# One block of small products instead of two, and a second product put off by a step, in a recurrence fused with a feed-forward layer

## The chip, the core and the metric

The kernel runs on one core of a Trainium2 chip. What counts is the device time of one execution in microseconds. The kernel before was timed three times: 566.85, 567.27 and 568.79 us, median 567.27 us.

## What is computed

The first half is a gated linear recurrence over 768 tokens, for 4 batches of 8 heads with 48 features; the second half is a feed-forward layer of width 2048 with an ELU between its two products. All of it is fp32.

```python
for t in range(S):                       # S = 768; q, k, v, f_logit: (4, 8, 768, 48)
    state = f[:, :, t, :, None] * state + np.einsum('bhd,bhe->bhde', k[:, :, t], v[:, :, t])
    y[:, :, t] = np.einsum('bhd,bhde->bhe', q[:, :, t], state)
...
h = x @ w_in                             # x: y as (3072, 384); w_in: (384, 2048)
g = np.where(h > 0.0, h, alpha * (np.exp(np.minimum(h, 0.0)) - 1.0))
return (g @ w_out).astype(np.float32)    # w_out: (2048, 384)
```

f is the sigmoid of f_logit.

## The kernel before

The function `fast` does the work; `general` is a fallback that is entered only when a flag, computed on the way, says that the inputs are out of range. Tokens are worked in twelve units of 256 (three to a batch, so units 0, 3, 6 and 9 begin a sequence), heads in pairs, and a unit's tokens in four chunks of 64.

The order of every engine's instructions is written out by hand. Time is counted in steps T, 16 to a unit, 192 in all. A table `plan` says which pieces of the recurrence are issued at which step, and the main loop at the end of `fast` adds the feed-forward layer around them:

- At an even step, `up(P)` issues the first product for one of the eight pairs of 128 hidden features of a unit, P = T/2. From unit 1 on this is `up7`, a scheme with seven products instead of eight (L882); it writes two banks, pa and pb, of a pair of PSUM buffers named "h". ScalarE copies a part of pa (L889), VectorE adds it to the rest (L891), and VectorE finishes the ELU of the pair before (L936). GpSimd makes sums of it for the second product (L946).
- At an odd step, `joined(P)` combines pb with it on VectorE (L904) and starts the exponential on ScalarE (L914, L915). Then come the planned pieces, and then `down(P - LAG)`, LAG = 2, the second product (L981), which accumulates over a unit's eight pairs in four PSUM banks, m0 to m3. Its first product of a unit goes to m0. After the eighth pair ScalarE and VectorE put the output together from these banks (L992, then five instructions of L991), and four transfers store it.

The recurrence of unit u works ahead of the feed-forward layer of unit u - 1. For u from 3 on, with t = 16(u - 1), the tuple A3 = (2, 4, 5, 7, 9, 11) gives the steps after t at which these are issued:

1. `transposed`: keys are transposed by TensorE (L669) into the banks a0 and a1, and copied out by ScalarE.
2. `advance`: 32 products of 64x48 (L728, 64 records in the trace) form each chunk's contribution to the state, into a0 and a1.
3. `step`: VectorE adds the contributions to the state chunk by chunk (L686), and for the last chunk multiplies by the decay (L691). In the first unit of a sequence the first of them is a copy on ScalarE (L688); in the last unit of a sequence the last is left out.
4. `scores`: 32 products of 64x64 of queries and keys (L705), into a0 and a1 again; `mask`: two VectorE instructions multiply them by the causal mask (L713).
5. `outputs`: masked scores by values (L743), into a0 and a1.
6. `carried`: queries by state (L763) on top; ScalarE copies the result out as the input of the feed-forward layer.

Each of `advance`, `scores`, `outputs` and `carried` is issued after an `up` or before it, in between full 128x128 products; the small products use a quarter of TensorE's array each.

Beside this, VectorE computes the decays of the next unit (L626, L631), and from step 52 on reduces a piece of the reread weights every fourth step (L603). During the first 76 us weights arrive as 64-bit numbers and are converted by VectorE and ScalarE (L563, L567, L573, L581) before the products that need them. A tile `fine`, 128x3, holds the range flags of the decays; `watch(u)` (L650) updates it once for each unit, for unit 1 at step 3. `warm` (L1032) issues products of the identity that nobody reads, to fill a hole on TensorE.

Of the kernel before, what the change touches and what calls it, by code (L numbers as in the profile page):

```python
# [356 lines left out]
def fast(ctx: ExitStack, tc: tile.TileContext, q, k, v, f_logit, w_in, w_out, out, flag, outer):  # L357
# [18 lines left out]
    nc = tc.nc  # L376
# [7 lines left out]
    NC = U // C  # L384
    UPB = S // U
    NU = B * UPB
    HP = H // 2
    NFT = DFF // 128
# [5 lines left out]
    LAG = 2  # L394
    AHEAD = 7
    WA = 1
    F1 = (1, 3)
    W0 = 3
    HOLD = 2
    A1 = (2, 5, 6, 8, 10, 11)  # L400
    D2 = (16, 18, 20, 22)
    A2 = (23, 25, 25, 26, 27, 28)
    D3 = (-7, -5, -3, -1)
    A3 = (2, 4, 5, 7, 9, 11)
    BL = 13
    RR = 0
    MX = 10
# [254 lines left out]
    def transposed(u, h, bank, pairs=(0, 1)):  # L662

        if 0 in pairs:
            pts[u, h] = ps.tile([128, 2, NW, 128], FP32, tag=bank, name=f"psT{u}_{h}")
            kns[u, h] = sb.tile([128, 2, NW, 128], FP32, tag="kn", name=f"kn{u}_{h}")
        for p in pairs:
            for w in range(NW):
                nc.tensor.transpose(  # L669
                    pts[u, h][:, p, w], in_=qkf[u % NB]["k"][:, 2 * h + p, w * W : (w + 1) * W], identity=ident[:]  # L670
                )
        p = slice(pairs[0], pairs[-1] + 1)
        nc.scalar.copy(kns[u, h][:, p], pts[u, h][:, p])
# [3 lines left out]
    def step(u, c):  # L677

        if u % UPB == UPB - 1 and c == NC - 1:
            return  # L680
        new = pus[u][c % 2][:, c // 2]
        box = boxes[(u * NC + c) % len(boxes)]
        s = box[:].rearrange("n (p d) -> n p d", d=64)[:, 0:HP, PAD:]
        if u % UPB or c:
            old = sts[u, c][:].rearrange("n (p d) -> n p d", d=64)[:, 0:HP, PAD:]
            nc.vector.tensor_tensor(out=s, in0=new, in1=old, op=ALU.add)  # L686
        else:
            nc.scalar.copy(s, new)  # L688
        if c == NC - 1:
            end = qkf[u % NB]["f"][:, :, 1, U - 1 :].broadcast_to([128, HP, D])  # L690
            nc.vector.tensor_tensor(out=s, in0=s, in1=end, op=ALU.mult)  # L691
        sts[(u, c + 1) if c < NC - 1 else (u + 1, 0)] = box

    def scores(u, banks=("a0", "a1"), pairs=range(HP), pc=None):

        t = qkf[u % NB]
        if pc is None:
            ats[u] = sb.tile([128, 2, NW, HP, C], FP32, tag="at", name=f"at{u}", bufs=1)
            pc = [ps.tile([128, NW, HP, C], FP32, tag=banks[r], name=f"psS{u}_{r}") for r in range(2)]
        for p in pairs:  # L700
            for w in range(NW):
                for b in range(2):
                    cols = slice(w * W + b * C, w * W + b * C + C)
                    for r in range(2):
                        nc.tensor.matmul(  # L705
                            pc[r][FULL[b], w, p], lhsT=t["k"][FULL[r], p, cols], rhs=t["q"][FULL[r], p, cols],
                            start=True, stop=True,
                        )
        return pc

    def mask(u, pc):
        for r in range(2):
            nc.vector.tensor_tensor(  # L713
                out=ats[u][:, r].rearrange("k w p i -> k (w p) i"), in0=pc[r][:].rearrange("k w p i -> k (w p) i"),
                in1=twice[:].unsqueeze(1).broadcast_to([128, NW * HP, C]), op=ALU.mult,
            )

    def advance(u, pairs=range(HP)):

        if u not in pus:  # L720
            pus[u] = [ps.tile([128, NW, HP, D], FP32, tag=n, name=f"psU{u}_{n}") for n in ("a0", "a1")]
        pu = pus[u]
        for p in pairs:
            for w in range(NW):
                for r in range(2):
                    h = 2 * p + r
                    for b in range(2):
                        nc.tensor.matmul(  # L728
                            pu[b][FULL[r], w, p], lhsT=kns[u, p // 2][FULL[b], p % 2, w, FULL[r]],
                            rhs=vs[u % NB][FULL[b], w, PAD + h * D : PAD + (h + 1) * D],  # L730
                            start=(w == 0 and p == 0), stop=(w == NW - 1 and p == HP - 1), skip_group_check=True,
                        )

    def outputs(u, banks=("a0", "a1")):


        pys[u] = [ps.tile([128, NW, HP, C], FP32, tag=banks[b], name=f"psY{u}_{b}") for b in range(2)]
        at = ats.pop(u)
        for w in range(NW):
            for p in range(HP):  # L740
                for r in range(2):
                    for b in range(2):
                        nc.tensor.matmul(  # L743
                            pys[u][b][FULL[r ^ b], w, p], lhsT=of_head(u, b, w, r, p),
                            rhs=at[FULL[b], r, w, p], start=(w == 0 and p == 0), stop=False,
                            skip_group_check=True,
                        )

        for b in range(2):
            nc.scalar.copy(between[:], pys[u][b][:, :, :, 0])  # L750

    def carried(u):

        t = qkf[u % NB]
        py = pys.pop(u)
        for w in range(NW):
            for p in range(HP):
                for b in range(2):
                    c = 2 * w + b
                    if (u % UPB, c) == (0, 0):  # L760
                        continue
                    for r in range(2):
                        nc.tensor.matmul(  # L763
                            py[b][FULL[r ^ b], w, p], lhsT=sts[u, c][FULL[r], 64 * p + r * PAD : 64 * (p + 1) + r * PAD],
                            rhs=t["q"][FULL[r], p, c * C : (c + 1) * C],
                            start=False, stop=True, skip_group_check=True,
                        )
        x = xts[u] = sb.tile([128, HP + 1, U], FP32, tag="xt", name=f"xt{u}", bufs=3)
        to = x[:, 0:HP].rearrange("n p (w b i) -> n b w p i", b=2, i=C)
        nc.scalar.copy(to[:, 0], py[0][:])  # L770
        for r in range(2):
            nc.scalar.copy(to[FULL[r], 1], py[1][FULL[1 - r]])
        for r in range(2):
            frm = PAD + D * r
            (nc.sync if u > 1 else nc.scalar).dma_start(
                out=x[GAP[r] : GAP[r] + PAD, 0:NKT], in_=x[frm : frm + D, NKT]
            )
# [46 lines left out]
    def at_step(step, *todo):  # L824
        plan.setdefault(step, []).extend(todo)

    def attention(u, first, then):

        kept = []
        for p, i in enumerate(first):  # L830
            at_step(i, (lambda: settle(u)) if p == NKT else lambda p=p: decays(u, p))
        if u > 1:
            at_step(then[0], lambda: transposed(u, 0, "a0"), lambda: transposed(u, 1, "a1"))
        at_step(then[1], lambda: advance(u))
        at_step(then[2], *(lambda c=c: step(u, c) for c in range(NC)))
        at_step(then[3], lambda: kept.append(scores(u)), lambda: mask(u, kept[0]))
        at_step(then[4], lambda: outputs(u))
        at_step(then[5], lambda: carried(u))

    gs, ss, pms, phs = {}, {}, {}, {}  # L840

# [187 lines left out]
        nc.tensor.matmul(pf[0:1, :], lhsT=low[:], rhs=causal[:, W - 1 : W], start=True, stop=True)  # L1029
        nc.vector.tensor_copy(flag[:], pf[0:1, :])  # L1030

    def warm(n, bank="m0"):  # L1032

        pw = ps.tile([128, 4, 128], FP32, tag=bank, name="psW")
        for _ in range(n):
            nc.tensor.matmul(
                pw[:], lhsT=ident[:], rhs=ident[:].unsqueeze(1).broadcast_to([128, 4, 128]), start=True, stop=True
            )
# [81 lines left out]
    at_step(F1[1], lambda: move(1, 1, nc.scalar), lambda: watch(1))  # L1120
    at_step(F1[1] + 2, lambda: scale(1, ("q", NKT, nc.gpsimd)))
    at_step(A1[0], lambda: transposed(1, 0, "a0"), lambda: transposed(1, 1, "a1"))
    attention(1, (), A1)
    at_step(8, lambda: load(2))
    at_step(14, lambda: gates(2))
# [8 lines left out]
    for u in range(3, NU):  # L1134
        t = (u - 1) * NFT
        at_step(t + BL, lambda u=u: blend(u))
        at_step(t - 16, lambda u=u: load(u))
        at_step(t - 8, lambda u=u: gates(u))
        attention(u, [t + i for i in D3], [t + i for i in A3])
    for n in range(NR):  # L1140
        t = 3 * NFT + (NU - 4) * NFT * n // NR + RR
        at_step(t, lambda n=n: reread(n))
# [3 lines left out]
    for T in range(NU * NFT):  # L1146
        P = T // 2
        sevens = order[P][0] >= DIRECT
        if T % 2 and sevens:
            joined(P)  # L1150
        if T % 2 == 0 and P and order[P - 1][0] < DIRECT:
            elu(P - 1)
        for f in plan.pop(T, ()):
            f()
        if T % 2 == 0:
            up(P)
        elif P >= LAG:
            down(P - LAG)
        for n in later.pop(T, ()):
            split(n)  # L1160
            lower(n)
# [53 lines left out]
```

## Time and profile before

| | us |
|---|---|
| median of three runs | 567.27 |
| lowest, highest | 566.85, 568.79 |
| profiled execution, span from its first to its last instruction | 567.3 |
| TensorE busy in it | 547.5 (97%) |
| VectorE busy | 409.4 (72%) |
| GpSimd busy | 292.7 (52%) |
| ScalarE busy | 230.2 (41%) |

Nothing of the profiled execution's time is shown outside of its span, so the span stands for its own time. In the page's second part each digit is the busy share of one fortieth of the span, in tenths. In the timeline a row gives the start and the length in us, the engine, the line of the kernel, the operation, the tiles that it writes and reads, shapes, and how many instructions of that kind follow one another; in brackets stands the idle time of the engine before it and what ended it. Matmuls are pipelined and their ends are modelled, so durations on TensorE are best taken from start to start. An fp32 product appears as two records.

### The profile page before, as it was taken

The page shows a single profiled execution, that of the slowest core. Times are in us where ns is not written, and L with a number is a line of the kernel's source. Part 1 is how long each engine was busy: PE and PEld are TensorE (multiplying, and loading weights), DVE is VectorE, ACT ScalarE, POOL GpSimd, SP SyncE. Part 2 cuts the span into 40 slices and gives each one's busy share as a digit, 9 for nine tenths or more (in the row PEclk, how much of TensorE's full clock was granted, in tenths as well). Part 3 has the DMA queues.
Part 4 walks back from the last instruction along what each step waited for, and adds up shares of the span by engine and source line. Part 5 has one row for each costly group of instructions (what it writes and reads, how often), then busy time and mean ns, then how long its engine had stood idle before and what let it go on. Part 6 is the DMA issues. An engine that isn't in the chain of part 4 may idle for free.

```text
span 567.3 us, 15527 instructions
## 1 busy us (share of the span) xinstructions
PE 547.5 (97%) x6336; PEld 509.7 (90%) x6336; DVE 409.4 (72%) x802; ACT 230.2 (41%) x424; POOL 292.7 (52%) x567
## 2 busy tenths in 40 slices
PE   6879998999999999999999999999999999999996
PEld 3566677999999999999999999999999999999996
DVE  8779989785675785885785885786776876745543
ACT  3287862443343433434343343333343343233331
POOL 6601788475374465456366357257248348325332
PEclk9899999999999999999999999999999999999999
DMA  8997951024024225215216216206206203201001
GB/s 212 266 261 209 298 129 43 3 47 114 3 46 138 65 52 145 79 42 156 78 36 155 86 38 153 86 19 173 84 14 178 84 6 74 84 2 36 29 2 35
DMA packets 38193, 53.30 MB, mean 94 GB/s; under 512 B 3712, under 2 KB 27936, under 8 KB 38112
## 3 DMA queue, kind: packets, MB, share of 16 engines
q1 hardware_dynamic: 37312, 51.62, 34.2%
q8 instruction: 52, 0.85, 0.7%
q10 hardware_dynamic: 800, 0.59, 0.4%
q14 instruction: 29, 0.24, 0.1%
HBM read 44.04 MB, written 4.72 MB: 86 GB/s over the span
## 4 chain that ended last, share of the span: by engine, by line
PE 81%; DMA 7%; DVE 7%; issue 2%; POOL 1%; ACT 1%; SPq 0%; DVEq 0%; ACTq 0%; POOLq 0%
PE psH L882 36%; PE psM L981 36%; DMA area<-in_moe_w_in_dram 4%; PE psS L705 2%; PE psY L743 2%; PE psY L763 2%; PE psU_a L728 2%; DVE f L631 2%; PE psT L669 1%; DMA xt<-xt 1%; DMA f<-f 1%; DVE f L626 1%; DMA k<-in_k_dram 1%; DVE bits L563 1%; DVE area L850 1%
## 5 line engine op out<-in xcount | busy, mean ns | idle before, releaser
L882 PE MATMUL psH<-xt,wi 128*128 128x128 f32 (+1 forms) x1056 | 195.0, 294 | 0.1
L946 POOL TENSOR_TENSOR sums<-gg 128x128 f32<-128x128 f32 x176 | 77.7, 462 | 214.5 <-DVE gg L936 205.9
L882 PEld LDWEIGHTS psH<-xt,wi 128*128 128x128 f32 x1056 | 149.5, 192 | 1.8 <-DVE hh L891 0.4
L914 ACT ACTIVATE gg<-hh 128x512 f32<-128x512 f32 x88 | 55.5, 631 | 232.0 <-DVE hh L904 154.6
L882 PE MATMUL psH<-xt,area 128*128 128x128 f32 x704 | 121.8, 275 | 1.3 <-DVE hh L904 1.0
L882 PEld LDWEIGHTS psH<-xt,area 128*128 128x128 f32 x704 | 106.5, 191 | 6.3 <-PE psH L882 1.3
L891 DVE TENSOR_TENSOR hh<-psH,u 128x256 f32<-128x256 f32 x88 | 37.1, 422 | 93.9 <-ACT u L889 93.9
L981 PE MATMUL psM<-area,sums 128*128 128x192 f32 x528 | 100.2, 326 | 0.0
L981 PEld LDWEIGHTS psM<-area,sums 128*128 128x128 f32 x528 | 88.2, 190 | 0.0
L981 PE MATMUL psM<-wo,gg 128*128 128x192 f32 x352 | 74.9, 335 | 0.0
L631 DVE RECIPROCAL f<-f 128x256 f32<-128x256 f32 x36 | 62.7, 1747 | 1.1
L936 DVE SCALAR_TENSOR_TENSOR gg<-gg,hh 128x512 f32<-128x512 f32 x88 | 61.9, 703 | 1.5 <-ACT gg L915 1.5
L915 ACT ACTIVATE gg<-gg 128x512 f32<-128x512 f32 x96 | 60.6, 631 | 3.0
L981 PEld LDWEIGHTS psM<-wo,gg 128*128 128x128 f32 x352 | 55.2, 190 | 2.0
L904 DVE TENSOR_TENSOR hh<-psH,u43h 128x256 f32<-128x256 f32 (+1 forms) x176 | 54.7, 352 | 3.0
L946 POOL TENSOR_TENSOR sums<-gg,sums 128x128 f32<-128x128 f32 x88 | 47.0, 534 | 6.9
L889 ACT COPY u<-psH 128x128 f32<-128x128 f32 x88 | 23.1, 263 | 60.9 <-PE psH L882 60.9
L621 POOL TENSOR_TENSOR q<-q,f 128x256 f32<-128x256 f32 x48 | 35.7, 745 | 21.8 <-DVE f L631 10.6
L904 DVE TENSOR_TENSOR u43h<-psH,hh 128x256 f32<-128x256 f32 x88 | 37.1, 422 | 12.7 <-PE psH L882 12.4
L621 POOL TENSOR_TENSOR k<-k,f 128x256 f32<-128x256 f32 x48 | 40.7, 851 | 7.1 <-DMA f<-f 5.1
L981 PE MATMUL psM<-area,gg 128*128 128x192 f32 x176 | 43.0, 326 | 0.0
L981 PE MATMUL psM<-wo,sums 128*128 128x192 f32 x176 | 43.0, 326 | 0.0
(97 smaller groups left out, 672.3 us busy)
## 6 DMA issues: line engine op xcount, KB each, us to landing
area<-in_moe_w_out_dram SPq DMA_DIRECT2D x8, 768.0 KB, 9.6
again<-in_moe_w_in_dram SPq DMA_DIRECT2D x16, 384.0 KB, 4.2
again<-in_moe_w_out_dram SPq DMA_DIRECT2D x16, 384.0 KB, 3.5
k<-in_k_dram SPq DMA_DIRECT2D x12, 384.0 KB, 4.5
q<-in_q_dram SPq DMA_DIRECT2D x12, 384.0 KB, 5.4
v<-in_v_dram SPq DMA_DIRECT2D x12, 384.0 KB, 5.8
area<-in_moe_w_in_dram SPq DMA_DIRECT2D x8, 576.0 KB, 8.4
out_dram<-o SPq DMA_DIRECT2D x42, 96.0 KB, 1.7
```

Of the source, the lines that this page charges most:

```text
L621: e.tensor_tensor(out=t[n][:, p], in0=t[n][:, p], in1=t["f"][:, p, "kq".index(n)], op=ALU.mult)
L631: nc.vector.reciprocal(f[:, p, 1], f[:, p, 0])
L705: nc.tensor.matmul(pc[r][FULL[b], w, p], lhsT=t["k"][FULL[r], p, cols], rhs=t["q"][FULL[r], p, cols], start=True, stop=True,)
L882: nc.tensor.matmul(to, lhsT=lhs, rhs=rhs, start=(n == 0), stop=True, skip_group_check=True)
L889: nc.scalar.copy(u1[:], pa[:, 0])
L891: add = lambda to, x, y: nc.vector.tensor_tensor(out=to, in0=x, in1=y, op=ALU.add)
L904: add = lambda to, x, y: nc.vector.tensor_tensor(out=to, in0=x, in1=y, op=ALU.add)
L914: nc.scalar.activation(g[:], h, AF.Relu, scale=-1.0)
L915: nc.scalar.activation(g[:], g[:], AF.Exp, scale=-1.0)
L936: nc.vector.scalar_tensor_tensor(out=g[:], in0=g[:], scalar=-1.0, in1=phs.pop(P), op0=ALU.add, op1=ALU.max)
L946: nc.gpsimd.tensor_tensor(out=s[:, i], in0=x, in1=y, op=op)
L981: nc.tensor.matmul(pm[bank][:, half * DH : (half + 1) * DH], lhsT=x, rhs=y, start=first, stop=(j == NP - 1), skip_group_check=True,)
```

## The change

- For units 3 to 11 except 8 (`APART`), a new function `both` issues `advance`, `scores`, `step` and `mask` together at step t + 5. A3 has four entries for them: 2, 5, 9, 11. Unit 8 keeps the six steps as before (`B3`).
- In these units the scores go into m3 (first half) and m0 (second half), two banks of the second product, instead of a0 and a1.
- At the step t + 5 of these units (`joint`) no `down` is issued. At t + 7 two are: the one put off, which is the first pair of a unit, and then the regular one.
- At step 4, `warm` gets a new argument: 31 products of one column by one column of `fine`, into bank m3, ahead of that step's `up`.

```diff
-    A3 = (2, 4, 5, 7, 9, 11)
+    A3 = (2, 5, 9, 11)
+    APART, B3 = 8, (2, 4, 5, 7, 9, 11)
...
+    SMALL = 31
...
+    def both(u):
+
+        advance(u)
+        pc = scores(u, ("m3", "m0"))
+        for c in range(NC):
+            step(u, c)
+        mask(u, pc)
+
     def attention(u, first, then):
...
-        at_step(then[1], lambda: advance(u))
-        at_step(then[2], *(lambda c=c: step(u, c) for c in range(NC)))
-        at_step(then[3], lambda: kept.append(scores(u)), lambda: mask(u, kept[0]))
-        at_step(then[4], lambda: outputs(u))
-        at_step(then[5], lambda: carried(u))
+        if len(then) == 4:
+            at_step(then[1], lambda: both(u))
+        else:
+            at_step(then[1], lambda: advance(u))
+            at_step(then[2], *(lambda c=c: step(u, c) for c in range(NC)))
+            at_step(then[3], lambda: kept.append(scores(u)), lambda: mask(u, kept[0]))
+        at_step(then[-2], lambda: outputs(u))
+        at_step(then[-1], lambda: carried(u))
...
-    def warm(n, bank="m0"):
+    def warm(n, bank="m0", small=0):

         pw = ps.tile([128, 4, 128], FP32, tag=bank, name="psW")
+        for _ in range(small):
+            nc.tensor.matmul(pw[0:1, 0, 0:1], lhsT=fine[:, 0], rhs=fine[:, 0], start=True, stop=True)
...
     at_step(A1[0], lambda: transposed(1, 0, "a0"), lambda: transposed(1, 1, "a1"))
+    at_step(4, lambda: warm(0, "m3", SMALL))
     attention(1, (), A1)
...
-        attention(u, [t + i for i in D3], [t + i for i in A3])
+        attention(u, [t + i for i in D3], [t + i for i in (B3 if u == APART else A3)])
+    joint = [(u - 1) * NFT + A3[1] for u in range(3, NU) if u != APART]
...
-        elif P >= LAG:
+        elif P >= LAG and T not in joint:
+            if T - 2 in joint:
+                down(P - LAG - 1)
             down(P - LAG)
```

## The prediction

> **What bounds the kernel now.** I read the page first: busy time in 40 slices, then the granted clock.
>
> ```profile
> PE   6879998999999999999999999999999999999996
> ...
> DVE  8779989785675785885785885786776876745543
> ...
> PEclk9899999999999999999999999999999999999999
> ```
>
> From the eighth slice on (about 100 us) TensorE is full at full clock; the windows view gives it 446.0 of the 446.0 us from 104 to 550. Whatever makes TensorE wait there is added to the span, whatever shortens its own work is taken off. Before 100 us it has holes (67.7 of 74.0 us busy from 30 to 104), with VectorE as the fuller engine. Next I read TensorE's timeline around a unit's stages; here the fifth unit (index 4), step by step:
>
> ```profile
> 179.60 1.15 PE L728 MATMUL psU_a<-v,kn 64*64 64x48 f32 x64
> 180.68 0.49 PE L882 MATMUL psH<-xt,wi 128*128 128x128 f32 x2
> ...
> 188.03 1.16 PE L705 MATMUL psS<-q,k 64*64 64x64 f32 x64
> 189.13 0.92 PE L981 MATMUL psM<-wo,gg 128*128 128x192 f32 x4
> ...
> 191.51 0.38 PE L882 MATMUL psH<-xt,wi 128*128 128x128 f32 x2
> ```
>
> The reader is to see a chain without holes: `advance` (L728) at E = 179.60, `up`, `down`, `up`, `scores` (L705), `down`, and the next `up` at E + 11.91. I call E the start of `advance`. The same stretch on VectorE:
>
> ```profile
> 180.14 0.36 DVE L991 TENSOR_TENSOR o<-psM,u 128x192 f32<-128x192 f32 x1 [1.63 <-ACT u L992]
> ...
> 184.70 0.62 DVE L904 TENSOR_TENSOR hh<-psH,u43h 128x256 f32<-128x256 f32 x2
> 185.24 1.52 DVE L686 TENSOR_TENSOR state<-psU_a,state 128x192 f32<-128x192 f32 x4
> 186.80 0.36 DVE L691 TENSOR_TENSOR state<-state,f 128x192 f32<-128x192 f32 x1
> ...
> 189.25 1.29 DVE L713 TENSOR_TENSOR at<-psS,twice 128x512 f32<-128x512 f32 x2
> ```
>
> It is behind: at this place it evacuates the finished unit's output (L991) and reduces a reread weight (L603, at 182.40), and only then reaches the step's own sums. From 180.14 to 187.16 it has no idle time, so nothing that TensorE delivers sooner makes it sooner. The mask (L713) comes 9.6 us after E, when nobody yet needs it.
>
> **What the skill says.** The Trainium skill, TensorEngine Tiling (Array Packing), Key Properties: changing the tiling mode drains TensorE. The trace agrees: an `up` takes 2.44 us start to start before a `down`, 2.53 before a block of 64x64 products; a `down` 2.28, and 2.38 after one. TensorE: Matmul & The Clock Gate, Architectural detail: ScalarE and VectorE are strict first-in first-out; the rows above stand in program order. PSUM — Partial Sum Buffer, Summary: while matmuls run, read a different bank, guarded by semaphores per bank; so a bank is handed on when its last reader has ended. In the built program of the change the first product of `down` waits for the second mask instruction.
>
> **The change, part by part.** Sums are made against the profiled execution's span, 567.3 us, equal to the median of the runs (567.27).
>
> *One block for two, eight units.* Two blocks cost 2 x (1.08 + 0.09 + 0.10) = 2.54 us: 1.08 start to start for 64 records (32 products), of which the weight loads' pace is 1.02. One block of 128 records costs 2.10 + 0.19 = 2.29. Gain 0.25 a unit, 2.0 us in all, if nothing waits. No instruction but the 31 small ones is added.
>
> *Scores in m3 and m0.* They are written after `up` (2.44) and `advance` (1.02), at E + 3.5. The last reads that hold these banks are the first two L991, ending by E + 1.4 (180.97). No wait.
>
> *The mask before `down`.* The new order on TensorE is up, advance + scores, up, down, down. Without waits the first of the two `down` starts at E + 7.1: -0.09 + 2.53 + 2.20 + 2.44. It writes m0, so now it needs both masks, and these stand in VectorE's queue behind everything shown above. In the fifth unit L691 ends at 187.16, the two masks take 1.28 with about 0.08 overlap: end at 188.36, E + 8.76. Add 0.1 from VectorE to TensorE (a merge ended at 38.54 and TensorE took it at 38.66). The two `down` take 4.56, so the next `up` starts at E + 13.42 where it was 11.91: +1.5 us. Inside this lies a wait of some 0.3 us: the second `up` wants a bank that L904 releases at E + 5.73 and it would reach it at 5.54. It is swallowed by the longer wait. Behind the waiting product stand both `down` and all later products; nothing passes it. VectorE's next sums move behind the mask, but are wanted only after two `down`.
>
> The same sum per unit, with mask end, new end and old end after E:
> - indices 4, 7, 10: 8.76, 13.42, 11.91: +1.5 each, 4.5.
> - 5 and 11 (three state sums, no L691): L686 ends at 230.12 with E = 223.35, mask end 7.97, 12.63 against 11.90: +0.7 each, 1.4.
> - 6 and 9 (a sequence's first unit): VectorE also waits for a ScalarE copy of the first state, queued there behind two activations:
>
> ```profile
> 274.43 1.14 DVE L686 TENSOR_TENSOR state<-psU_a,state 128x192 f32<-128x192 f32 x3 [1.62 <-ACT state L688]
> ```
>
>   With E = 267.09 the mask ends at 10.08, 14.74 against 12.00: +2.7 each, 5.5.
> - 3 (that copy too, but no L603 yet): 9.27, 13.93 against 11.90: +2.0.
>
> Sum +13.4 us, the 2.0 gained already inside. Nothing later gives it back, as TensorE has no idle time after 104 us. The buffers of the postponed `down` (gg of four, sums of three) are not asked for before it runs. Bounds from 0.3 us either way per unit: 11 to 16.
>
> *31 products of 1x1.* They are queued before the third `up` and read `fine`; in the built program they wait for the L650 that step 3 issues.
>
> ```profile
> 33.63 2.76 PE L927 MATMUL psH<-xt,wi 128*128 128x256 f32 x12
> 38.69 2.83 PE L927 MATMUL psH<-xt,wi 128*128 128x256 f32 x12 [2.30 <-DVE wi L581]
> ```
> ```profile
> 40.52 1.75 DVE L631 RECIPROCAL f<-f 128x256 f32<-128x256 f32 x1
> 42.18 0.10 DVE L650 SCALAR_TENSOR_TENSOR fine<-f,fine 128x3 f32<-128x3 f32 x1
> ```
>
> So TensorE stands from 36.4 to 42.3 instead of 38.7: +3.6 us. The nearest row for the products themselves is the flag's:
>
> ```profile
> 550.16 0.19 PE L1029 MATMUL psF<-causal,low 128*1 128x1 f32 x2
> ```
>
> One fp32 product is two records, 0.02 us apart. 62 records at 20 ns are 1.2 us; at the 62 ns of the skill's TensorE page (Back-to-back issue gap, the slower decode) 3.8, an estimate. I take 2.5. The same page says (Part 1) that a window of about 3.4 us idle halves the clock; the trace agrees in kind, with a granted clock of 0.50 from 24.6 to 27.9 us (windows view) after holes among small products. A hole of 5.9 us may bring one more; I add 0.1, at most 1.7. So the third `up` ends about 6.2 us late. Behind it queue `advance`, the first `down` and all of TensorE; ScalarE's activation of that `up` (45.45) and the next lowering behind it are late too. TensorE's later holes up to 63 us (0.7 + 0.2 + 0.2 + 0.6) end on VectorE or ScalarE work that moves less: they take 1.7. Those from 78 to 99 us (0.3 + 0.5 + 0.5 + 0.9) hang on chains that TensorE's lateness moves as well; I let them take about 1. Left +3.5, bounds 0 (all hidden behind the weights' merging) and 7.5.
>
> Total: 567.3 + 13.4 + 3.5 = 584.2 us.
>
> **Rivals.** (a) *The saved drains decide*, not slower: the mask is done before TensorE asks. Place: the eight joined blocks; price -2.0 us, time 565.3 with the early wait hidden in the 3.9 us of holes. It decides from a mask end under E + 7.1; the rows give 7.97 to 10.08 on an engine without idle time, so it would need VectorE's chain 1 to 3 us shorter. (b) *The early wait is hidden*: the first 76 us are paced by weights and merges. 580.7. Against: ScalarE and VectorE wait for the late `up` in program order. (c) *The early wait grows*: half clock over two windows and slow small products, 588. (d) *No wait on the mask* in effect, only the early one: 567.3 - 2.0 + 3.5 = 568.8. Against: the built program's semaphore. That the change doesn't do what it says is excluded by the built order.
>
> **How the numbers follow.** Forecast 0.68; (b) 0.13; (c) 0.08; (d) 0.05; (a) 0.04; a tie 0.02. The forecast's own bounds, 11 to 16 with 0 to 6, are not all met at once: 578 to 589 covers it with (b) and (c). What a measurement can tell from no change is about 0.3%, 1.7 us: faster 0.04, same 0.02, slower 0.94.
>
> **What would show it.** In the profile after: before the first of two adjoining `down`, TensorE idle released by VectorE's mask, 0.6 to 2.7 us, eight times, longest in units 6 and 9; the joined block 2.1 us; the ninth unit as before; the third `up` starting near 45 us and the 104 us point 3 to 4 us later. I am wrong if the mask ends before the second `up` does, if the small products start before 42 us, or if TensorE waits for something else after 104 us.

## The result and the profile after

The changed kernel takes 588.40 us (median of six runs, 585.52 to 590.60). The kernel before, timed beside it, takes 567.96 us (six runs, 566.85 to 568.79). The ratio is 1.0361, 95% interval 1.0335 to 1.0388: 20.4 us slower. The prediction was 584.2 us, range 578 to 589: it is right in direction, 4.2 us short, and the result lies near the upper end of its range.

The profiled execution after has a span of 588.3 us, where 567.3 was before: 21.0 more. Its own time is 590.2 us, and in all executions on record the time is 1.7 to 1.9 us above the span. So a span does not stand for the time of its execution, as was assumed above for the kernel before; here spans are compared with spans and times with times. First the page's 40 slices, as before (PE is TensorE, DVE is VectorE, ACT is ScalarE, PEclk is the granted clock of TensorE in tenths of full speed):

```profile
PE   7759999999899999999899999999899999999996
...
DVE  8577979785675785785685786786767768645543
PEclk9887999999999999999999999999899999999999
```

TensorE is no longer full after 100 us: the slices 147 to 162, 279 to 294 and 412 to 426 us fall to 8. The granted clock has new dips in the third and fourth slice (29 to 59 us) and in the 29th (412 to 426 us). What TensorE waited for, in microseconds in all, times, and longest:

```profile
PE psM L994 <- DVE at L715: 11.6, 8, 2.5
PE psW L1049 <- DVE fine L652: 6.0, 1, 6.0
```

Neither wait existed before. Eight waits of `down` (L994, L981 before) for the mask (L715, L713 before), and one of the small products (L1049) for the range flags (L652, L650 before). Other lines have moved too: L895 and, in the first unit, L940 are `up`, L730 is `advance`, L707 `scores`, L688 and L693 `step`, L1004 the output, L605 the reductions of the reread weights. Unit index 4 on TensorE:

```profile
189.11 1.15 PE L730 MATMUL psU_a<-v,kn 64*64 64x48 f32 x64
190.08 1.14 PE L707 MATMUL psS<-q,k 64*64 64x64 f32 x64
...
192.54 0.68 PE L895 MATMUL psH<-xt,area 128*128 128x128 f32 x4 [0.23 <-DVE hh L917]
...
193.94 0.39 PE L895 MATMUL psH<-xt,wi 128*128 128x128 f32 x2
195.55 0.92 PE L994 MATMUL psM<-wo,gg 128*128 128x192 f32 x4 [1.23 <-DVE at L715]
...
200.21 0.38 PE L895 MATMUL psH<-xt,wi 128*128 128x128 f32 x2
```

The two small stages now adjoin. After the second `up` TensorE waits 1.23 us, then both `down` run. VectorE in the same stretch:

```profile
187.21 0.36 DVE L1004 TENSOR_TENSOR o<-psM,u 128x192 f32<-128x192 f32 x1 [1.63 <-ACT u L1005]
...
192.31 1.59 DVE L688 TENSOR_TENSOR state<-psU_a,state 128x192 f32<-128x192 f32 x4
193.94 0.36 DVE L693 TENSOR_TENSOR state<-state,f 128x192 f32<-128x192 f32 x1
194.22 1.28 DVE L715 TENSOR_TENSOR at<-psS,twice 128x512 f32<-128x512 f32 x2
```

The mask ends at 195.50 and the first product of `down` starts at 195.55. From 187.21 to 195.50 VectorE has no idle time: it is not slow at the mask, it comes to it last. The scores had been finished since about 191.2.

A unit's cost is read from the start of its transposes to the start of the next unit's. For units 3 to 10 this was 43.73 to 43.83 us before; after it is 45.70, 45.38, 44.58, 46.62, 45.37, 43.75, 48.21 and 45.37. With the end (0.8 more behind unit 11's transposes) that adds 15.7 us. Between unit 1 and unit 2 it is 68.94 instead of 64.46: 4.5. Of the remaining 0.8 of the 21.0 us, 0.7 lies ahead of unit 1 (33.47 instead of 32.76), where the code is the same; this start-up took 30.3 to 33.5 us in the executions profiled here, so it is scatter.

### The profile page after: what moved, and what is told of

The parts are those of the page before. It is cut to its first block, busy times and chain, and to the rows that moved or that the text cites. A ratio compares the mean times of both kernels' runs of the same rounds, so it can differ in the third digit from the quotient of the medians.

```text
span 588.3 us, 15648 instructions
## 1 busy us (share of the span) xinstructions
PE 553.8 (94%) x6398; PEld 514.5 (87%) x6398; DVE 407.7 (69%) x802; ACT 230.2 (39%) x424; POOL 291.5 (50%) x567
## 4 chain that ended last, share of the span: by engine, by line
PE 80%; DVE 10%; ACT 4%; issue 2%; DMA 1%; POOL 1%; SPq 0%; ACTq 0%; DVEq 0%; POOLq 0%
PE psM L994 35%; PE psH L895 31%; PE psH L940 2%; PE psY L745 2%; PE psS L707 2%; PE psY L765 2%; PE psU_a L730 2%; DVE at L715 2%; DVE f L633 2%; DVE state L688 2%; ACT area L575 2%; PE psT L671 1%; PE psM L972 1%; DMA f<-f 1%; DVE hh L917 1%
## 5 line engine op out<-in xcount | busy, mean ns | idle before, releaser
L895 PE MATMUL psH<-xt,wi 128*128 128x128 f32 (+1 forms) x1056 | 194.9, 293 | 0.0
L895 PEld LDWEIGHTS psH<-xt,wi 128*128 128x128 f32 x1056 | 149.5, 192 | 1.5
L895 PE MATMUL psH<-xt,area 128*128 128x128 f32 x704 | 122.3, 276 | 2.5 <-DVE hh L917 2.0
L895 PEld LDWEIGHTS psH<-xt,area 128*128 128x128 f32 x704 | 106.5, 191 | 8.5 <-PE psH L895 3.3
L904 DVE TENSOR_TENSOR hh<-psH,u 128x256 f32<-128x256 f32 x88 | 37.1, 422 | 109.8 <-ACT u L902 109.8
L994 PE MATMUL psM<-area,sums 128*128 128x192 f32 x528 | 101.1, 328 | 0.0
L994 PEld LDWEIGHTS psM<-area,sums 128*128 128x128 f32 x528 | 89.1, 192 | 0.0
L994 PE MATMUL psM<-wo,gg 128*128 128x192 f32 x352 | 75.6, 338 | 11.6 <-DVE at L715 11.6
L994 PEld LDWEIGHTS psM<-wo,gg 128*128 128x128 f32 x352 | 56.1, 192 | 14.5 <-DVE at L715 13.1
L917 DVE TENSOR_TENSOR hh<-psH,u43h 128x256 f32<-128x256 f32 (+1 forms) x176 | 54.7, 353 | 3.0
L917 DVE TENSOR_TENSOR u43h<-psH,hh 128x256 f32<-128x256 f32 x88 | 37.2, 422 | 12.2 <-PE psH L895 11.4
L623 POOL TENSOR_TENSOR k<-k,f 128x256 f32<-128x256 f32 x48 | 39.3, 822 | 8.5 <-DMA f<-f 6.0
L994 PE MATMUL psM<-area,gg 128*128 128x192 f32 x176 | 43.0, 326 | 0.0
L994 PE MATMUL psM<-wo,sums 128*128 128x192 f32 x176 | 43.0, 326 | 0.0
```

Source lines behind the costliest of these rows:

```text
L623: e.tensor_tensor(out=t[n][:, p], in0=t[n][:, p], in1=t["f"][:, p, "kq".index(n)], op=ALU.mult)
L895: nc.tensor.matmul(to, lhsT=lhs, rhs=rhs, start=(n == 0), stop=True, skip_group_check=True)
L904: add = lambda to, x, y: nc.vector.tensor_tensor(out=to, in0=x, in1=y, op=ALU.add)
L917: add = lambda to, x, y: nc.vector.tensor_tensor(out=to, in0=x, in1=y, op=ALU.add)
L994: nc.tensor.matmul(pm[bank][:, half * DH : (half + 1) * DH], lhsT=x, rhs=y, start=first, stop=(j == NP - 1), skip_group_check=True,)
```

## The experiments

Theory M: the mask's place at the end of VectorE's queue makes `down` wait, and this is nearly the whole slowdown per unit; the flags cost the rest early. Rivals: the order of TensorE's blocks or the two adjoining `down` cost by themselves; the small products cost by their number and not by what they wait for; the lower clock is the cause. Edits are against the changed kernel, except where the kernel before is named. "Beside it" is the kernel before on the same chip.

**no_small: without the small products.**

```diff
-    at_step(4, lambda: warm(0, "m3", SMALL))
```

> The changed kernel without the 31 products of 1x1. Theory (the wait for the flags costs what the trace shows up to the first unit's stages, 5.1 us, and the eight joined blocks cost 14.1 us with or without it): 583 us, 15 us above the kernel before, and TensorE busy without a hole from 36 to 42 us beyond the 2.3 us of before. Rival (the early lateness is hidden behind the merging of weights, and the joined blocks cost all): 588 us as the changed kernel.

Measured: 584.19 us, beside it 568.45, ratio 1.0280 (1.0244 to 1.0315). In the profile unit 1 to unit 2 takes 64.22 us, as before, and the units 45.70, 45.37, 44.58, 46.61, 45.37, 43.75, 46.61 and 45.37. So the small products are not what slows the later units. Nor is the lower clock: from its first instruction to the last 0.7 us of the span the clock in this profile is full. Unit 9 is 1.6 us shorter here than in the changed kernel, which comes back below.

**small_only: the kernel before with the small products, and nothing else of the change.**

```diff
+    at_step(4, lambda: warm(0, "m3", 31))
```

> The kernel before with the 31 products of 1x1 and nothing else of the change. Theory: 568 + 5.1 = 573 us, with a hole of 6 us before the small products and half clock for the third up after it. Rival (hidden): 568 us.

Measured: 572.28 us, beside it 568.45, ratio 1.0075 (1.0052 to 1.0098), or 4.3 us. In the profile the wait for the flags is 6.0 us, unit 1 to unit 2 takes 68.33 us (3.9 more), and the clock is halved from 39.1 us on for 6.8 us. The two parts add up: by their ratios 15.9 (no_small) and 4.3 us (small_only), 20.2 together, against 20.4 for the whole change.

**small_ident: the same 31 products in the kernel before, of a tile that is there from the start.**

```diff
-            nc.tensor.matmul(pw[0:1, 0, 0:1], lhsT=fine[:, 0], rhs=fine[:, 0], start=True, stop=True)
+            nc.tensor.matmul(pw[0:1, 0, 0:1], lhsT=ident[:, 0:1], rhs=ident[:, 0:1], start=True, stop=True)
```

> The kernel before with the same 31 products of 1x1, but of a column of the identity, which is there from the start, so that they wait for nothing on VectorE. Theory (the wait costs, the products don't): they take 1.6 us inside the 2.3 us hole before the third up, 568 us, no half clock at 40 us. Rival (the products themselves or the switch of tile shape cost): 569.5 us or more.

Measured: 568.16 us, beside it 568.45, ratio 0.9991 (0.9973 to 1.0009). Its TensorE:

```profile
35.39 1.69 PE L1036 MATMUL psW<-ident 128*1 128x1 f32 x62
37.76 2.83 PE L927 MATMUL psH<-xt,wi 128*128 128x256 f32 x12 [0.69 <-DVE wi L581]
```

The products lie inside a hole that was there anyway and end before the weights come. Here their number costs nothing; what costs is the operand that they wait for.

**mask_first: no_small, and the mask issued ahead of the state sums.**

```diff
         pc = scores(u, ("m3", "m0"))
+        mask(u, pc)
         for c in range(NC):
             step(u, c)
-        mask(u, pc)
```

> The changed kernel without the 31 products, with the mask issued on VectorE ahead of the state sums of the same step. Theory (TensorE waits only for the mask's place in VectorE's queue): the masks end about 7.0 us after the old start of advance, before TensorE is through with the second up (7.1 to 7.4), so the eight waits before down vanish. Left are the saved block switches, -2.0 us, and the wait of 0.25 to 0.5 us in the second up for a bank of the first, in seven units, +2 to +3: 567 to 569 us, about the kernel before (567.9). Rival (the waits come from the joined block itself, from the postponed down or from its banks): stays near 583 us.

Measured: 568.36 us, beside it 567.77, ratio 1.0013 (1.0002 to 1.0023). The whole slowdown per unit is gone. Unit index 4 on TensorE, the end of the second `up` and the first `down`:

```profile
183.36 0.68 PE L895 MATMUL psH<-xt,area 128*128 128x128 f32 x4 [0.24 <-DVE hh L917]
...
184.75 0.39 PE L895 MATMUL psH<-xt,wi 128*128 128x128 f32 x2
184.98 0.82 PE L994 MATMUL psM<-wo,gg 128*128 128x192 f32 x4
```

and its VectorE:

```profile
183.12 1.28 DVE L715 TENSOR_TENSOR at<-psS,twice 128x512 f32<-128x512 f32 x2
184.32 1.53 DVE L688 TENSOR_TENSOR state<-psU_a,state 128x192 f32<-128x192 f32 x4
```

The mask ends at 184.40, TensorE gets to `down` at 184.98 and doesn't wait. The list of TensorE's waits holds no L994 at all. The adjoining `down`, the block of 128 records and the banks m3 and m0 are all still there, so none of them is the cause. The units take 43.40 (index 3) and 43.87 to 43.89, the ninth 43.75. What keeps the other seven from the saving is the wait in the second `up`, which the long wait had covered: pb is released by L917 (L904 before), which here stands behind a reduction of reread weights (L605).

**mask_first_rr2: mask_first, and the rereads with these reductions two steps later.**

```diff
-    RR = 0
+    RR = 2
```

> As the one with the mask first, and the rereads with their reductions two steps later, so that the reduction of 1.0 us falls behind the masks and not ahead of them. Theory: the wait in the second up vanishes too, and the saved block switches alone are left: 567.9 - 2.0 = 566 us. Rival (the block switches aren't worth 0.25 us each, or the moved reduction delays something else): 567.9 us or more.

Measured: 565.80 us, beside it 567.77, ratio 0.9969 (0.9955 to 0.9983). The wait in `up` is gone and the units take 43.40 to 43.55, the ninth 43.75:

```profile
180.32 1.15 PE L730 MATMUL psU_a<-v,kn 64*64 64x48 f32 x64
181.29 1.14 PE L707 MATMUL psS<-q,k 64*64 64x64 f32 x64
182.36 0.49 PE L895 MATMUL psH<-xt,wi 128*128 128x128 f32 x2
```

So one block instead of two saves 43.75 - 43.41 = 0.34 us a unit once nothing waits, and the second wait had cost 43.88 - 43.41 = 0.47.

**no_small_rr2: no_small, and only the rereads with their reductions later; the mask stays last.**

```diff
-    RR = 0
+    RR = 2
```

> The changed kernel without the 31 products, mask still last, but the rereads' reductions two steps later, so that their 1.0 us falls behind the masks in seven of the eight units. Theory (a unit's wait is what VectorE's queue holds ahead of the mask): 0.9 us a unit off in units that wait at least so long (4, 6, 7, 9, 10), less in 5 and 11 where the wait is 0.4 us plus 0.5 in the second up, none in unit 3: 583 - 6 = 577 us, and the waits of the second up vanish. Rival (the wait is fixed by the state sums or ScalarE's copy): 583 us.

Measured: 577.43 us, beside it 568.07, ratio 1.0177 (1.0140 to 1.0214). The seven units after the first joined one are each 0.9 us shorter than in no_small (index 4: 44.45 instead of 45.37), the first, which has no such reduction, is as long (45.69). Two reductions take 1.00 us with their overlap. Taking work from ahead of the mask shortens the wait by that work: this is what a queue in order does, and what a fixed price of the new block order would not.

**swap_banks: no_small, with the halves of the scores exchanged.**

```diff
-        pc = scores(u, ("m3", "m0"))
+        pc = scores(u, ("m0", "m3"))
```

> The changed kernel without the 31 products, with the two score banks exchanged: the first mask then frees m0, which the first product of down writes, and the second mask frees m3, which its second product writes. Theory (TensorE waits for the masks, in VectorE's order): the first product starts up to 0.6 us sooner, the second still waits for the second mask, so a unit gains one product, 0.33 us at most: 583 - 2.6 = 580 to 581 us. Rival (the wait is VectorE's lateness as a whole, or a wait for something else that comes with the postponed down): 583 us.

Measured: 581.85 us, beside it 568.45, ratio 1.0244 (1.0206 to 1.0283). Each joined unit is 0.32 or 0.33 us shorter than in no_small, but for unit index 9, where a stretch of half clock adds 1.7. The first product of `down` now wants only the first mask instruction, the second product (m3) the second; so one product (two records, 0.33 us from start to start) comes out of the wait. In unit index 4 it falls from 1.23 to 0.63 us ahead of the first product, and about 0.3 us of it returns ahead of the second: the row of the first four records of `down` is 1.19 us long, not 0.92.

**filled: no_small, with 31 products of the identity put into the hole in three units (indices 3, 6 and 9).**

```diff
             if T - 2 in joint:
+                if T // NFT in (2, 5, 8):
+                    warm(0, "m1", SMALL)
                 down(P - LAG - 1)
```

The operand is changed as in small_ident.

> The changed kernel without its 31 early products, and with 31 products of 1x1 of the identity (into m1, idle there) issued in each of the three longest waits, those of the units 3, 6 and 9, ahead of the two downs: they take 1.7 us of a wait of 2 to 2.6 us and leave the masks' order as it is. Theory (in some executions a window of half clock follows such a wait, 1.6 us each, since the windows run free and the wait falls differently into them): the median comes down from 584 to 580.5 to 582 us, and the profile has no half clock after 104 us. Rival (the difference between the runs of that kernel and its profile of 578.5 us span lies elsewhere): 584 us.

Measured: 583.97 us, beside it 568.57, ratio 1.0264 (1.0243 to 1.0285). Unit index 6:

```profile
277.65 1.69 PE L1049 MATMUL psW<-ident 128*1 128x1 f32 x62
280.21 1.65 PE L994 MATMUL psM<-wo,gg 128*128 128x192 f32 x4 [0.86 <-DVE at L715]
```

Its windows view: time from and to, length, busy time of TensorE, its weight loads, VectorE, ScalarE, GpSimd, then granted clock, DMA share, GB/s:

```profile
280.20:283.40 3.20, 3.19 (x10) 3.20 (x11) 2.75 (x7) 1.21 (x3) 1.75 (x4) 0.50 0.00 0
```

The idle time of the hole is down to 0.86 us, and yet the clock is halved after it and the four records take 1.65 us instead of 0.92. One-column products did not avert it. So the run can't decide between its two expectations: the time stayed at the rival's 584 us, but the half clock that was to be taken away was still there.

**no_small_again: no_small once more, for the clock.**

> The changed kernel without its 31 early products once more, beside the one with filled waits on the same chip. Theory: 580 to 584 us, with zero, one or two windows of half clock of 1.6 us in its profile after 104 us, and a span longer by as much than the 578.5 us of the profile that had none. Rival: a longer span without such a window.

Measured: 584.48 us, beside it 568.57, ratio 1.0277 (1.0257 to 1.0296). After 100 us this profile has one stretch at half clock while TensorE works, in unit index 6 (48.03 us instead of 46.61), and one before, at 36.7 us; the first profile had none. The time of the profiled execution is 580.3 us in the first and 582.4 here, and both lie under the medians, 584.2 and 584.5. More such stretches in the other executions would explain that. Their mean granted clock is on record and fits: 0.999 in the profiled execution of no_small, 0.990 to 0.996 in its four others, which have spans 4.0 to 4.2 us longer. Where their stretches lay is not on record.

**all_units: mask_first_rr2, with the ninth unit joined too.**

```diff
-    APART, B3 = 8, (2, 4, 5, 7, 9, 11)
+    APART, B3 = 0, (2, 4, 5, 7, 9, 11)
```

> As the one before, with the ninth unit joined as well. Theory: another 0.25 us, 565.7 us. Rival (the ninth unit has something that the others don't, which is why it was left out): at or above the one before.

Measured: 565.43 us, beside it 567.77, ratio 0.9956 (0.9939 to 0.9973). The ninth unit takes 43.41 instead of 43.75. This version has the lowest median, 2.3 us under the kernel before; its interval overlaps that of mask_first_rr2.

**all_units_ident: all_units, with the 31 products of the identity at step 4.**

```diff
+    at_step(4, lambda: warm(0, "m3", SMALL))
```

The operand is changed as in small_ident.

> The fastest version so far (mask first, reductions later, all nine units) with the 31 small products put back, of a column of the identity instead of the flags, so that they fill the hole before the third up and wait for nothing. Theory (holes among the first 100 us are covered by the merging of weights, a half clock there too): no change, 565.4 us. Rival (the hole costs by a window of half clock, which the small products avert): about 1 us less.

Measured: 566.09 us, beside it 568.07, ratio 0.9964 (0.9954 to 0.9975): no difference from all_units that is clear of the intervals. The clock is halved from 37.3 us on all the same, as it is from 39.7 us on in all_units, so the products did not avert it; what a half clock costs there is not shown by this pair.

## Why the prediction was right, point by point

The prediction had 16.9 us more, 13.4 for the mask and 3.5 for the small products; 20.4 were measured. In the profile the two are 15.7 and 4.5. Both mechanisms came as foretold and both were sized too low, most of all by a clock that is halved after a long wait. That the median comes close to rival (c)'s 588 us is luck: (c) put all of its 3.8 us early, where 1.0 us came; the larger part of what was missing came in the later units. The sum also set a span (567.3 us) equal to a time, while the time is some 1.8 us above its span; the forecast difference doesn't depend on that.

*The mask before `down`: right in place and nearly in size.* The prediction put the mask's end in unit index 4 at E + 8.76 and the next `up` at E + 13.42. By its sum the joined block starts at E + 2.44; it starts at 189.11, so E is 186.67 after. The mask ends at E + 8.83 and the next `up` starts at E + 13.54. Per unit, predicted and measured in the profile after:

| unit index | predicted | measured |
|---|---|---|
| 3 | +2.0 | +1.97 |
| 4, 7, 10 | +1.5 | +1.63, +1.63, +1.62 |
| 5, 11 | +0.7 | +0.83, +0.83 |
| 6 | +2.7 | +2.79 |
| 8 | 0 | +0.01 |
| 9 | +2.7 | +4.38 |

The sum is 15.7 where 13.4 was predicted. Unit 9 alone makes 1.7 of the difference. The idle times ahead of `down` are 0.44 to 2.49 us, where 0.6 to 2.7 was foretold. mask_first shows the cause by taking it away; no_small_rr2 and swap_banks show its size by taking away 0.9 and 0.33.

*Unit 9: a term that was missing.* The prediction had no half clock after 100 us. Here is the first `down` of unit 6 and of unit 9 on TensorE, and for unit 9 the windows ahead of it and after it:

```profile
286.76 0.92 PE L994 MATMUL psM<-wo,gg 128*128 128x192 f32 x4 [2.49 <-DVE at L715]
...
422.50 1.65 PE L994 MATMUL psM<-wo,gg 128*128 128x192 f32 x4 [2.49 <-DVE at L715]
```
```profile
419.00:422.20 3.20, 1.01 (x8) 0.77 (x6) 2.39 (x6) 0.84 (x3) 0.05 (x1) 1.00 0.68 234
422.40:425.70 3.30, 3.20 (x10) 3.21 (x11) 2.85 (x8) 1.21 (x3) 1.74 (x4) 0.50 0.00 0
```

After 2.5 us of waiting the clock is 0.50 for one window of 3.4 us, and the two `down` take 6.24 us instead of 4.66: the 1.6 us by which this unit exceeds its counterpart, unit 6. Unit 6 has a wait as long and keeps its clock. Within an execution half-clock windows begin at whole multiples of 3.413 us from each other (in this trace at 19.58, 40.06 and 422.35 us, 6 and 112 times 3.413 us apart). Counted on from the one at 422.4, unit 6's hole (284.3 to 286.8) has a boundary in it at 285.8, which leaves 1.6 and 0.9 us idle in two windows, and unit 9's (420.0 to 422.5) lies in one window but for its last 0.2 us. No experiment moved a hole against the windows; the six timed executions of the changed kernel fit, as the shortest (585.52 us) has the highest mean clock, 0.991, and the longest two 0.984 and 0.985.

*The small products: right in cause, short in size, 4.5 us where 3.5 was predicted.* They start at 43.05, and the third `up` starts at 44.67 ("near 45"). The terms:

```profile
34.34 2.75 PE L940 MATMUL psH<-xt,wi 128*128 128x256 f32 x12
43.05 1.69 PE L1049 MATMUL psW<-fine 128*1 128x1 f32 x62 [5.96 <-DVE fine L652]
44.67 5.49 PE L940 MATMUL psH<-xt,wi 128*128 128x256 f32 x12
50.09 1.22 PE L730 MATMUL psU_a<-v,kn 64*64 64x48 f32 x64
```
```profile
40.10:44.60 4.50, 1.55 (x62) 1.55 (x62) 4.47 (x7) 3.59 (x6) 0.99 (x1) 0.50 1.06 252
44.70:50.20 5.50, 5.50 (x18) 3.96 (x20) 4.33 (x7) 1.73 (x2) 0.62 (x1) 0.50 0.50 138
```

The wait is 5.96 us (5.9 predicted). The products take 1.62 us up to the next start, not 2.5: their records are 25 ns apart, near the 20 ns read from the flag's row and not the 62. The half clock was put at 0.1, at most 1.7; it lasts three windows, 40.1 to 50.3, and the third `up` takes 5.42 us from start to start where it took 2.76 before (38.69 to 41.45), so it costs 2.7. `advance` starts 8.6 us later than before, 7.9 without the 0.7 of the start-up, where 6.2 was predicted. Of these 7.9 the later holes absorb 3.4 (2.7 predicted), and 4.5 is left. So the mis-sized term is the half clock. It is one half of rival (c), with three windows in place of two; its other half, slow small products, did not come. The 4.5 left is inside the bounds of 0 to 7.5.

*Block switches: 0.34 us a unit, predicted 0.25.* The joined block takes 2.04 us from start to start in mask_first_rr2, not 2.10; that is 0.06 of the 0.09. In the changed kernel the saving is inside the sums above.

*The second `up`: a wait of 0.24 us in the row, 0.47 in the unit.* The prediction saw it (some 0.3) and rightly called it swallowed. When the longer wait was removed, it showed at once. The row's idle time is counted from the modelled end of the product before, and the slip of the starts is larger: in mask_first 183.36 follows 182.51 by 0.85 us, and in mask_first_rr2 the same two rows follow by 0.44 (182.91, 183.35).

*Rivals.* (a) and (d) needed the mask to be early. It wasn't. mask_first_rr2 has it early and is near to what (a) described, with the small products out and the reductions moved: 2.0 us of saving worked out, 567.77 - 565.80 = 1.97 measured, 0.8 to 2.6 by the interval. The close agreement is luck, as a unit saves 0.34 us and not 0.25. (b) falls by small_only, 4.3 us. Rival (d), at 568.8, was counted with the slower outcomes, though it is 1.5 us above the kernel before and the prediction put what can be told apart at 1.7.

*The clock's windows.* The Trainium skill, TensorE: Matmul & The Clock Gate, Part 1, has a free-running window of about 3.4 us and a halved clock after a window without work. The windows agree: stretches at half clock while TensorE works last 3.41 us or two or three times that. That a whole window must be idle does not hold here: 2.3 idle us of 3.41 in the window ahead of unit 9's `down` were enough (with the boundaries as above), and 1.8 of 3.41 were not, in the kernel before (34.8 to 38.2 us). Idle time alone does not settle it: in the kernel before 1.5 us (21.1 to 24.6 us, among small products) were enough, and in no_small_rr2 1.9 us (141.8 to 145.2 us) were not. The measurement decides; what exactly is counted in a window stays open.

## What to carry to other kernels

Before work is moved into banks that another product accumulates in, look at the last reader's place in its engine's queue, not only at its length: here 1.28 us of mask stood behind what VectorE still had to do, and moving it ahead of the state sums brought 584.2 down to 568.4 us. Then look for the wait that the long one hid; here it ate the whole saving until a reduction was moved. Work meant to fill a hole must not depend on something later than the hole's end.

## What the runs showed of the hardware

- A wait of 2.5 us on TensorE can cost 1.4 to 1.6 us more than itself: the clock was halved in the next window in unit 9 of the changed kernel, not in unit 6, and in unit 6 of no_small_again, not in no_small. With the boundaries counted as above, the window that took most of the hole had 2.3 and 2.0 us idle where the clock was halved, and 1.6 and 1.5 us where it was not.
- Sixty-two records of one column fill 1.7 us and count as busy in the view, but the clock was halved after them in filled (280.2 us) and in all_units_ident (37.3 us). Counted as idle, they would leave 2.4 and 2.3 us idle of the 3.41 us ahead, and 1.8 us in small_ident, where the clock stayed full. That they don't count as work for the clock is argued from this, not shown.
- Sixty-two such records last 1.69 us at half clock (changed kernel) and 1.69 us at full clock (small_ident), in both 25 ns from start to start. The twelve records of 128x256 of the third `up` took 5.42 us at half clock and 2.76 at full clock.
